# Three more key units and four more tiles as float16 pairs, and a running maximum read from PSUM

## The chip, the cores and the metric

The kernel runs on one core of one Trainium2 chip. The metric is the device time of one execution in microseconds; several executions are timed and their median is compared. One more execution is recorded with the hardware profiler, and the trace comes from that one.

## The reference

Agent attention over four batches of 11456 tokens with 128 features and 49 agents, and after it a mixture of eight experts, of which each token takes one. In short:

```python
scale = 1 / sqrt(128)
a2k = softmax(scale * agents @ k.T)          # 49 x 11456, per batch
agent_v = a2k @ v                            # 49 x 128
x = softmax(scale * q @ agents.T) @ agent_v  # 11456 x 128
e = argmax(normalized(x) @ normalized(expert_emb).T / tau)
g = softmax(...)[e]
out = g * (relu(x @ w1[e]) @ w2[e])          # w1: 128 x 1024, w2: 1024 x 128
```

All inputs and outputs are float32.

## The kernel before

**Units and tiles.** A batch is cut into 12 units: 11 of 128 partitions x 8 tokens and a rest of 96 x 2. A unit of keys, values or queries is loaded by one DMA of 512 KB on SP's queue. The second part of the kernel works in tiles of half a unit: 23 a batch, numbered t from 0, of 4 columns x 128 tokens each, the last one smaller. Batches are numbered b from 0, so the second batch is b = 1.

**Keys.** For each unit the scores of keys and agents are computed, kept in SBUF (tile s_u, filled by ACT), and a running maximum m_run over the units is kept by DVE. When all units of a batch are in, the maximum is made final (`k_max`), and then the value units use the kept scores (`k2_unit`). There are two ways for a unit. `k1_f32` transposes the keys on TensorE in float32 (line 436, 8 transposes into two PSUM banks), copies them to SBUF (lines 439 on DVE and 441 on ACT), multiplies with the agents in float32 (line 449; 16 matmuls a unit, of which the trace has two records each), copies the scores on ACT (473) and takes the maximum from PSUM on DVE (416). `k1_pairs` splits the keys into a float16 pair, value and residual, after a scaling by a power of two: ACT squares and sums them (490), DVE makes the scale (248, 250, 252), ACT writes the scaled value (494), DVE the residual (502). A DMA on SP's queue transposes both (507), and TensorE does three float16 matmuls for each of 8 columns (516 to 518). ACT copies the scores with the inverse scale (522), and the maximum is taken from that copy. Batches 0 and 1 use `k1_f32` alone. Of batches 2 and 3 `by_pairs` (line 1640) sends the even units through `k1_pairs`, the odd ones through `k1_f32`.

**Score banks.** Scores, routing sums and value sums go through a PSUM pool of two banks (tag s), and the transposes, the first layer and the proofs (vp) through one of four (tag h).

**Expert layers.** All tokens of a batch take, as far as can be proved, one expert, and what that expert does is folded beforehand (`pick_expert`) into small tables of that batch: gh and gl for the first layer, w2p for the second, lin for a linear part. Making them is a chain through ACT, DVE, TensorE and POOL, which runs beside the tiles of the batch before. For each tile and each of two blocks f, `ffn_mm1` does the first layer into an hp bank (1237, 1238) and the ReLU; `ffn_mm2` adds the second layer into yp. A tile is either a pair tile (ACT writes the float16 value, line 1246, DVE its residual, 1247; three float16 matmuls for each of 4 columns, 1273 to 1275) or a plain one (ACT writes float32, 1242; one float32 matmul for each column, 1270, two records each). `plain` (line 1223) makes tiles 16 and later plain, in all batches but the last.

**Order of the work.** The instructions are emitted by generators that a loop over ticks steps through, 4 ticks a tile, 92 a batch. `plan` gives due times to the key, value and query units: the keys of batch 2 begin at 0.30 of batch 0's ticks and those of batch 3 at 0.30 of batch 1's, spread evenly over 0.76 of a batch. From the emitted program a planner with estimated costs and priorities makes the order of each engine; SP's queue alone keeps the order of emission. Two buffers hold split keys (`h_slots`), three hold transposed ones (`x_slots`).

Of the kernel before, what the change touches and what calls it, by code (L numbers as in the profile page):

```python
# [14 lines left out]
ALU = mybir.AluOpType  # L15
# [14 lines left out]
def kernel(ctx: ExitStack, tc: tile.TileContext, q, k, v, agents, emb, tau, w1, w2, out):  # L30
    nc = tc.nc
    pe, dve, act, pool, sp = nc.tensor, nc.vector, nc.scalar, nc.gpsimd, nc.sync

    B, N, C = q.shape
    A = agents.shape[1]
    E, D, F = w1.shape
# [8 lines left out]
    BRISK = 4  # L45
    KEEP = 5
    LATE = 16

    REM_J, REM_P = 2, 96
    J = (N - REM_J * REM_P) // P  # L50
    TJ = 4
# [38 lines left out]
    def pss(name):  # L90
        return ps_s.tile([P, 512], F32, name=name, tag="s")
# [14 lines left out]
    def take(o, uses=1):  # L106
        at = o.asked
        o.asked += 1
        while len(o.left) < at or (at >= o.n and o.left[at - o.n]):
            yield 1  # L110
        o.left.append(uses)
        return at

    def give(o, i):
        o.left[i] -= 1
# [15 lines left out]
    def used(*unit):  # L131

        ring[slot[unit]][1] = now[0]
# [12 lines left out]
    def ushape(u):  # L146
        return (P, min(UJ, J - u * UJ)) if u < NU - 1 else (REM_P, REM_J)
# [94 lines left out]
    def half_scale(ssq, kexp, tag, bufs=2, bias=float(254 * ONE)):  # L242

        p = ssq.shape[0]
        sc = sm.tile([P, 1], F32, name="hsc", tag=tag + "c", bufs=bufs)[:p]
        iv = sm.tile([P, 1], F32, name="hiv", tag=tag + "i", bufs=bufs)[:p]
        si = sc.bitcast(I32)
        dve.tensor_scalar(si, ssq.bitcast(I32), -0.5, (190.5 + kexp) * ONE, ALU.mult, ALU.add)
        yield 1
        dve.tensor_scalar(si, si, EXPONENT, None, ALU.bitwise_and)  # L250
        yield 1
        dve.tensor_scalar(iv.bitcast(I32), si, -1.0, bias if isinstance(bias, float) else bias[:p], ALU.mult, ALU.add)
        return sc, iv
# [131 lines left out]
    def in_place(last):  # L385

        return tc.issue_after(last[-1].ins) if last else nullcontext()
# [20 lines left out]
    def blk_of(b, u):  # L408
        return [kb for kb in batches[b].blks if u in kb.us][0]

    def run_max(kb, spv, p, n):
        mr = kb.m_run[:p, :n, :]
        if kb.k1 + kb.us.start == 0:
            dve.tensor_copy(mr, spv)
        else:
            dve.tensor_tensor(out=mr, in0=spv, in1=mr, op=ALU.max)
# [61 lines left out]
    def k1_pairs(b, u):  # L478

        kb = blk_of(b, u)  # L480
        p, n = ushape(u)
        while ("k", b, u) not in units:
            yield 1
        src = units["k", b, u]
        kb.at[u] = yield from take(s_slots)
        j = yield from take(h_slots)
        sq = sm.tile([P, 1], F32, name="ksq", tag="ksq", bufs=3)[:p]
        xs = wk.tile([P, UJ, 2, D], F16, name="ks", tag="xs", bufs=XS)
        with in_place(h_last):
            act.activation(xs[:p, :n, 0], src[:p, :n], AF.Square, accum_out=sq)  # L490
        yield 1
        sc, iv = yield from half_scale(sq, 14, "ku", 4, kbias)
        with in_place(h_last):
            act.activation(xs[:p, :n, 0], src[:p, :n], AF.Copy, scale=sc)
        yield 1
        if u % 2:
            pool.tensor_tensor(out=src[:p, :n], in0=src[:p, :n], in1=sc.unsqueeze(2).broadcast_to([p, n, D]), op=ALU.mult)
            pool.tensor_tensor(out=xs[:p, :n, 1], in0=src[:p, :n], in1=xs[:p, :n, 0], op=ALU.subtract)
        else:
            for c in range(0, n, TJ):  # L500
                cs = slice(c, min(c + TJ, n))
                dve.scalar_tensor_tensor(out=xs[:p, cs, 1], in0=src[:p, cs], scalar=sc, in1=xs[:p, cs, 0], op0=ALU.mult, op1=ALU.subtract)
        used("k", b, u)
        yield 6
        i = yield from take(x_slots)
        kT = wk.tile([P, 2 * UJ, P], F16, name="kT", tag="xT", bufs=XB)
        sp.dma_start_transpose(out=kT[:, : 2 * n, :p], in_=xs[:p, :n].rearrange("p c h d -> p (c h d)"))
        yield 4
        give(h_slots, j)
        yield 1  # L510
        s = pss("sp")
        with in_place(y_last):
            for c in range(n):
                o = s[:p, c * A : (c + 1) * A]
                hi, lo = kT[:, 2 * c, :p], kT[:, 2 * c + 1, :p]
                pe.matmul(out=o, lhsT=hi, rhs=a16[:, b, :A], start=True, stop=False)
                pe.matmul(out=o, lhsT=hi, rhs=a16[:, b, A:], start=False, stop=False)
                pe.matmul(out=o, lhsT=lo, rhs=a16[:, b, :A], start=False, stop=True)
        give(x_slots, i)
        st = wk.tile([P, UJ, A], F32, name="s_u", tag="s_u", bufs=NU)[:p, :n]  # L520
        spv = s[:p, : n * A].rearrange("p (c a) -> p c a", a=A)
        act.activation(st, spv, AF.Copy, scale=iv)
        run_max(kb, st, p, n)
        kb.s[u] = st
        kb.k1 += 1

# [694 lines left out]
    live, yps = {}, {}  # L1221

    def plain(b, t):
        return b < B - 1 and t >= LATE

    def ffn_mm1(b, t, f):
        bt = batches[b]
        if plain(b, t) and not hasattr(bt, "w2f"):
            bt.w2f = sm.tile([P, 2, D], F32, name="w2f", tag="w2f", bufs=1)
            dve.tensor_tensor(out=bt.w2f, in0=bt.w2p[:, :, 0], in1=bt.w2p[:, :, 1], op=ALU.add)  # L1230
        u, w = unit_of(t)
        p, n = tshape(t)
        m = p * n
        tt = tts[b, u][:, w * TJ * P : w * TJ * P + m]
        hp = psh("hp")
        fs = slice(f * P, (f + 1) * P)
        pe.matmul(out=hp[:, :m], lhsT=bt.gh[:, fs], rhs=tt, start=True, stop=False)  # L1237
        pe.matmul(out=hp[:, :m], lhsT=bt.gl[:, fs], rhs=tt, start=False, stop=True)  # L1238
        h2 = wk.tile([P, 2, TJ * P], F16, name="hh", tag="hh", bufs=5)
        if plain(b, t):  # L1240
            hf = h2.rearrange("p h m -> p (h m)").bitcast(F32)
            h_last[:] = [act.activation(hf[:, :m], hp[:, :m], AF.Relu)]
            live[b, t, f] = (hf, None)
            return
        hh, hl = h2[:, 0], h2[:, 1]
        h_last[:] = [act.activation(hh[:, :m], hp[:, :m], AF.Relu)]  # L1246
        dve.scalar_tensor_tensor(out=hl[:, :m], in0=hp[:, :m], scalar=0.0, in1=hh[:, :m], op0=ALU.max, op1=ALU.subtract)  # L1247
        live[b, t, f] = (hh, hl)
# [389 lines left out]
        return sorted(kv), qs  # L1638

    def by_pairs(b, u):  # L1640
        return u % 2 == 0 and b > 1

    LEADS = {'k': 12, 'v': 9, 'q': 18}

# [13 lines left out]
    def keys():  # L1658

        start = now[0] // 2  # L1660
        for at, kind, b, u in plan()[0]:
            while now[0] // 2 < start + at:
                yield 1
            if kind == "k":
                if not hasattr(batches[b], "blks"):
                    k_start(b)
                spawn((k1_pairs if by_pairs(b, u) else k1_f32)(b, u))
            else:
                kb = batches[b].blks[0]
                if u == 0:  # L1670
                    while kb.k1 < NU:
                        yield 1
                    yield from k_max(b, pss, 1)
                    yield 1
                spawn(k2_unit(b, u, pool, (3, 4)))
                if u == NU - 1:
                    spawn(after_keys(b))
# [20 lines left out]
    with tc.manual_schedule(engines={mybir.EngineType.SP}):  # L1698
# [9 lines left out]
        for i in range(len(ticks) + LAG):  # L1708
            if i < len(ticks):
                b, t, r = ticks[i]  # L1710
# [12 lines left out]
            while due and due[0][0] <= i:  # L1723
                _, b, t, f = due.pop(0)
# [49 lines left out]
```

## Time and profile before

| what | value |
|---|---|
| median of 3 runs | 668.01 us (667.16 to 668.66) |
| profiled execution, its own time | 664.34 us |
| its span, first to last instruction | 662.6 us |
| TensorE (PE) busy | 631.3 us, 95% of the span |
| VectorE (DVE) busy | 513.8 us, 78% |
| ScalarE (ACT) busy | 458.7 us, 69% |
| GpSimd (POOL) busy | 345.7 us, 52% |
| mean granted TensorE clock | 0.996 |

The span is that of the instructions in the profiled execution; its own time has a little around it. The shares are averages over stages that differ. The end of a PE record is modelled and matmuls are pipelined, so the cost of a stream of matmuls is read from the starts of its records, not from their lengths.

### The profile page before, as it was taken

The numbers are of one execution on the slowest core, as the hardware profiler recorded it, in microseconds if no ns is written. First come the engines' busy times: TensorE is split into PE (matmuls) and PEld (weight loads), VectorE is DVE, ScalarE is ACT, GpSimd is POOL, SyncE is SP. The second block draws the span as 40 slices with busy tenths as digits, with TensorE's granted clock in tenths as the row PEclk, the third lists the DMA queues.
The fourth block names the chain that finished last, engine by engine and source line by source line (L and its number), as shares of the span: only waits on it lengthen the run. The fifth ranks groups of instructions, "written<-read, shape, count | busy, mean of one in ns | idle before, by whom it ended". The sixth has DMA issues, their size and how long they took to land. (4 is left out here: it accounts for less than half of the span.)

```text
span 662.6 us, 23329 instructions
## 1 busy us (share of the span) xinstructions
PE 631.3 (95%) x9299; PEld 540.1 (82%) x9299; DVE 513.8 (78%) x1487; ACT 458.7 (69%) x1147; POOL 345.7 (52%) x592
## 2 busy tenths in 40 slices
PE   8988999999999999999999889999999999999996
PEld 6887878888887877888888787888888897787886
DVE  5777798687776898876786889986576979896793
ACT  3537846877678956886777965876479855987642
POOL 6003284386135566783623684684655755877310
PEclk9989999999999999999999999999999999999999
DMA  8997397599686249999859455998568434314422
GB/s 341 286 348 212 57 342 194 125 226 286 180 265 188 64 118 217 285 295 230 216 182 245 120 114 147 264 282 217 130 196 216 102 65 138 62 34 137 142 101 76
DMA packets 157049, 123.33 MB, mean 186 GB/s; under 512 B 76753, under 2 KB 133155, under 8 KB 156939
## 3 DMA queue, kind: packets, MB, share of 16 engines
q1 hardware_dynamic: 143499, 97.97, 58.8%
q10 hardware_dynamic: 13120, 23.47, 10.2%
q8 instruction: 74, 1.21, 0.8%
q0 software_dynamic: 320, 0.38, 0.2%
q14 instruction: 36, 0.29, 0.1%
HBM read 80.26 MB, written 23.79 MB: 157 GB/s over the span
## 5 line engine op out<-in xcount | busy, mean ns | idle before, releaser
L1098 ACT ACTIVATE vp<-vp 128x512 f32<-128x512 f32 x180 | 106.4, 591 | 17.3 <-PE vp L1089 15.0
L1246 ACT ACTIVATE hh<-hp 128x512 f16<-128x512 f32 (+1 forms) x142 | 83.1, 592 | 47.9 <-PE hp L1238 32.6
L1247 DVE SCALAR_TENSOR_TENSOR hh<-hp,hh 128x512 f16<-128x512 f32 (+1 forms) x142 | 95.5, 676 | 26.3 <-ACT hh L1246 25.6
L1274 PE MATMUL yp<-w2p,hh 128*128 128x128 f16 x564 | 107.3, 219 | 0.0
L1273 PE MATMUL yp<-w2p,hh 128*128 128x128 f16 x564 | 107.0, 219 | 0.0
L1275 PE MATMUL yp<-w2p,hh 128*128 128x128 f16 x564 | 105.6, 219 | 0.3 <-DVE hh L1247 0.3
L449 PE MATMUL sp<-aT_all,fT 128*64 128x49 f32 x2496 | 95.9, 224 | 1.9 <-DVE vm L910 1.0
L449 PEld LDWEIGHTS sp<-aT_all,fT 128*64 128x64 f32 x2496 | 83.8, 137 | 15.9 <-issue 4.6
L441 ACT COPY fT<-fTp 128x512 f32<-128x512 f32 (+1 forms) x115 | 62.9, 572 | 31.1 <-PE fTp L436 20.7
L961 POOL TENSOR_TENSOR e<-qe,e 128x392 f16<-128x392 f32 (+1 forms) x48 | 43.0, 897 | 64.2 <-ACT e L958 53.0
L1237 PE MATMUL hp<-tt,gh 128*128 128x512 f16 (+1 forms) x184 | 68.7, 373 | 4.0 <-DVE hh L1247 1.8
L1089 PE MATMUL vp<-vm,tt 128*128 128x256 f16 x360 | 69.7, 273 | 0.7 <-DVE vmin L1095 0.6
L1036 POOL TENSOR_TENSOR nrm<-qq,half 128x16 f32<-128x16 f32 (+2 forms) x28 | 69.0, 2464 | 0.2
L1289 DVE TENSOR_TENSOR ot<-yp,gs 128x512 f32<-128x512 f32 (+1 forms) x92 | 61.5, 670 | 9.2 <-PE yp L1275 5.3
L1238 PE MATMUL hp<-tt,gl 128*128 128x512 f16 (+1 forms) x184 | 68.6, 373 | 0.0
L1261 PE MATMUL yp<-lin,tt 128*128 128x128 f16 x720 | 62.4, 219 | 2.2 <-DVE ot L1289 2.1
L1273 PEld LDWEIGHTS <-hh 128*128 128x128 f16 x564 | 55.4, 98 | 6.4 <-issue 0.7
L1275 PEld LDWEIGHTS <-hh 128*128 128x128 f16 x564 | 55.4, 98 | 6.1 <-DVE hh L1247 0.4
L1274 PEld LDWEIGHTS <-hh 128*128 128x128 f16 x564 | 55.5, 98 | 4.8 <-issue 0.5
L1261 PEld LDWEIGHTS <-tt 128*128 128x128 f16 x720 | 48.4, 99 | 9.9 <-issue 4.4
L997 POOL TENSOR_TENSOR rt<-rt 128x384 f32<-128x384 f32 (+1 forms) x48 | 40.7, 848 | 29.0 <-DVE rt L994 14.1
L436 PE MATMUL fTp<-ident,qt 128*128 128x128 f32 x360 | 54.2, 281 | 0.9 <-ACT vp L1098 0.4
(372 smaller groups left out, 1636.7 us busy)
## 6 DMA issues: line engine op xcount, KB each, us to landing
kt<-in_k_dram SPq DMA_DIRECT2D x44, 512.0 KB, 6.5
vt<-in_v_dram SPq DMA_DIRECT2D x44, 512.0 KB, 6.4
qt<-in_q_dram SPq DMA_DIRECT2D x44, 512.0 KB, 5.4
out_dram<-ot ACTq DMA_DIRECT2D x88, 256.0 KB, 3.5
w1s<-in_moe_w_dram SPq DMA_DIRECT2D x9, 512.0 KB, 4.2
w2s<-in_moe_w_dram SPq DMA_DIRECT2D x9, 512.0 KB, 5.3
tt<-e SPq DMA_TRANSPOSE x48, 4.6
kt<-in_k_dram SPq DMA_DIRECT2D x4, 96.0 KB, 8.5
```

The lines of the kernel that those rows point to most:

```text
L449: pe.matmul(out=s[h : h + w, c * A : (c + 1) * A], lhsT=xT[:, c * p + h : c * p + h + w], rhs=aT_all[:, b, :], start=True, stop=True, skip ...
L1036: pool.tensor_tensor(out=nrm, in0=quad, in1=half[:, :n], op=ALU.pow)
L1089: pe.matmul(out=z[:p, i * FP : (i + 1) * FP], lhsT=tt[:, c * p : (c + 1) * p], rhs=bt.vm[:, NEAR:], start=True, stop=True)
L1098: act.activation(z[:p], z[:p], AF.Relu, scale=-1.0, accum_out=bt.vsum[:p, at : at + 1])
L1237: pe.matmul(out=hp[:, :m], lhsT=bt.gh[:, fs], rhs=tt, start=True, stop=False)
L1238: pe.matmul(out=hp[:, :m], lhsT=bt.gl[:, fs], rhs=tt, start=False, stop=True)
L1246: h_last[:] = [act.activation(hh[:, :m], hp[:, :m], AF.Relu)]
L1247: dve.scalar_tensor_tensor(out=hl[:, :m], in0=hp[:, :m], scalar=0.0, in1=hh[:, :m], op0=ALU.max, op1=ALU.subtract)
L1261: pe.matmul(out=yp[:p, c, :], lhsT=tc_, rhs=bt.lin[:, h], start=(c == 0 and h == 0), stop=False, skip_group_check=True)
L1273: pe.matmul(out=y, lhsT=hh[:, cs], rhs=wh, start=False, stop=False, skip_group_check=True)
L1274: pe.matmul(out=y, lhsT=hh[:, cs], rhs=wl, start=False, stop=False, skip_group_check=True)
L1275: y_last[:] = [pe.matmul(out=y, lhsT=hl[:, cs], rhs=wh, start=False, stop=last, skip_group_check=True)]
```

## The change

Three edits. `MORE` names three odd units, unit 3 of batch 2 and units 3 and 7 of batch 3, which now go through `k1_pairs`; the branch of `k1_pairs` for odd units, which would have made the residual on POOL, goes, so all residuals are made on DVE. In `k1_pairs` the running maximum is taken from the scores in PSUM, scaled in the same instruction, and not from ACT's copy. And in batch 1 plain tiles begin at tile 20, so tiles 16 to 19 become pair tiles.

```diff
+    MORE = {2: (3,), 3: (3, 7)}
...
-        if u % 2:
-            pool.tensor_tensor(out=src[:p, :n], in0=src[:p, :n], in1=sc.unsqueeze(2).broadcast_to([p, n, D]), op=ALU.mult)
-            pool.tensor_tensor(out=xs[:p, :n, 1], in0=src[:p, :n], in1=xs[:p, :n, 0], op=ALU.subtract)
-        else:
-            for c in range(0, n, TJ):
-                cs = slice(c, min(c + TJ, n))
-                dve.scalar_tensor_tensor(out=xs[:p, cs, 1], in0=src[:p, cs], scalar=sc, in1=xs[:p, cs, 0], op0=ALU.mult, op1=ALU.subtract)
+        for c in range(0, n, TJ):
+            cs = slice(c, min(c + TJ, n))
+            dve.scalar_tensor_tensor(out=xs[:p, cs, 1], in0=src[:p, cs], scalar=sc, in1=xs[:p, cs, 0], op0=ALU.mult, op1=ALU.subtract)
...
         act.activation(st, spv, AF.Copy, scale=iv)
-        run_max(kb, st, p, n)
+        mr = kb.m_run[:p, :n, :]
+        if kb.k1 + kb.us.start == 0:
+            dve.tensor_scalar(mr, spv, iv, None, ALU.mult)
+        else:
+            dve.scalar_tensor_tensor(out=mr, in0=spv, scalar=iv, in1=mr, op0=ALU.mult, op1=ALU.max)
...
     def plain(b, t):
-        return b < B - 1 and t >= LATE
+        return b < B - 1 and t >= (LATE + 4 if b == 1 else LATE)
...
     def by_pairs(b, u):
-        return u % 2 == 0 and b > 1
+        return b > 1 and (u % 2 == 0 or u in MORE[b])
```

## Rows read from the trace of the kernel before

**Rows 1.** Busy us by stretch: PE, PEld, DVE, ACT, POOL; clock, DMA.
```profile
160.00:180.00 20.00, 20.00 (x318) 16.99 (x316) 15.09 (x36) 14.17 (x36) 6.37 (x12) 1.00 0.88 226
320.00:340.00 20.00, 20.00 (x338) 17.58 (x333) 16.70 (x38) 14.98 (x37) 8.94 (x11) 1.00 0.71 195
350.00:370.00 20.00, 19.01 (x245) 16.41 (x245) 12.15 (x43) 16.00 (x39) 9.68 (x13) 1.00 0.95 243
365.00:380.00 15.00, 12.96 (x155) 10.20 (x154) 12.58 (x29) 14.97 (x30) 10.36 (x11) 1.00 0.43 109
```

**Rows 2.** Timeline of ACT: start and length in us, then the instruction.
```profile
169.70 0.49 ACT L473 COPY s_u<-sp 128x392 f32<-128x392 f32 x1 [1.54 <-PE sp L449]
...
326.68 0.49 ACT L473 COPY s_u<-sp 128x392 f32<-128x392 f32 x1 [0.36 <-PE sp L449]
...
345.32 0.63 ACT L1242 ACTIVATE hh<-hp 128x512 f32<-128x512 f32 x1
...
363.57 0.61 ACT L1242 ACTIVATE hh<-hp 128x512 f32<-128x512 f32 x1
...
376.65 0.47 ACT L473 COPY s_u<-sp 128x392 f32<-128x392 f32 x1
```

**Rows 3.** Timeline of PE; 17 single rows stand between 360.24 and 360.71.
```profile
351.81 0.60 PE L436 MATMUL fTp<-ident,kt 128*128 128x128 f32 x4
352.25 0.55 PE L1261 MATMUL yp<-lin,tt 128*128 128x128 f16 x7
352.73 1.14 PE L449 MATMUL sp<-aT_all,fT 128*64 128x49 f32 x32
353.80 0.38 PE L258 MATMUL total<-wsq,ones 128*128 128x1 f32 x2
...
360.24 0.18 PE L516 MATMUL sp<-a,kT 128*128 128x49 f16 x1
...
360.71 0.38 PE L1237 MATMUL hp<-tt,gh 128*128 128x512 f16 x1
...
361.81 1.06 PE L1270 MATMUL yp<-w2f,hh 128*128 128x128 f32 x8
362.71 0.61 PE L1261 MATMUL yp<-lin,tt 128*128 128x128 f16 x8
363.15 0.38 PE L1237 MATMUL hp<-tt,gh 128*128 128x512 f16 x1
```

**Rows 4.** Busy us by stretch for tile ks (split keys) alone: DVE, ACT.
```profile
130.00:140.00 10.00, 1.42 (x2) 2.28 (x3) 1.00 0.75 207
...
370.00:380.00 10.00, 2.39 (x2) 0.68 (x1) 1.00 0.09 33
```

**Rows 5.** Groups by form: count, busy us, mean ns, idle before and its releaser.
```profile
L1247 DVE SCALAR_TENSOR_TENSOR hh<-hp,hh 128x512 f16<-128x512 f32 x140 | 94.8, 681 | 26.1 <-ACT hh L1246 25.6
...
L441 ACT COPY fT<-fTp 128x512 f32<-128x512 f32 x107 | 60.3, 591 | 30.5 <-PE fTp L436 20.7 <-PE hp L1238 3.0 <-DVE vmin L1171 1.8
...
L473 ACT COPY s_u<-sp 128x392 f32<-128x392 f32 x32 | 15.4, 485 | 16.0 <-PE sp L449 16.0
...
L522 ACT ACTIVATE s_u<-sp,hiv 128x392 f32<-128x392 f32 x12 | 7.1, 592 | 3.7 <-PE sp L518 3.7
```

**Rows 6.** The running maximum: its two groups by form; who waited for it.
```profile
L416 DVE TENSOR_TENSOR m_run<-sp,m_run 128x392 f32<-128x392 f32 x28 | 15.7, 562 | 12.3 <-ACT s_u L473 12.2
...
L416 DVE TENSOR_TENSOR m_run<-s_u,m_run 128x392 f32<-128x392 f32 x12 | 9.0, 746 | 1.1 <-ACT s_u L522 0.9
...
  PEld sp L449: 1.6, 3
```

**Rows 7.** What the first matmuls of pair units (L516) waited for.
```profile
  DMA kT<-ks: 3.1, 3
```

**Rows 8.** Waits of SP's queue: us in total, times, longest.
```profile
SPq L507 <- PE hp L1238: 17.5, 2, 11.5
```

**Rows 9.** Timeline of PE at the change to the third batch.
```profile
397.67 0.38 PE L1237 MATMUL hp<-tt,gh 128*128 128x512 f16 x1 [1.79 <-DVE hh L1247]
```

## The prediction

> **What bounds the kernel now.** I read the busy time by stretches first. TensorE (PE) is busy 20.00 of 20 us in 160 to 180 and in 320 to 340, while DVE and ACT have 3 to 6 us of rest [rows 1]: there the time is PE's instruction stream, and a microsecond of matmuls less is a microsecond less. It isn't so everywhere. In 365 to 380 ACT is busy 14.97 of 15 us and PE only 12.96 [rows 1]: this is the end of the second batch's second layer, where the third batch's expert is being picked. So each part of the change has to be placed before it is priced, and the second view is the ACT timeline, which dates the parts [rows 2]: the score copy (L473) of the third batch's unit 3 stands at 169.70, of the fourth batch's unit 3 at 326.68 and of its unit 7 at 376.65; the first ReLU of the second batch's tile 16 stands at 345.32, and of its tile 18 at 363.57. Then come the pitches of the PE instructions, by the starts of merged rows [rows 3], and the price of the same work on ACT and DVE [rows 4, 5].
>
> **The three units, on PE.** A float32 unit issues 8 transposes and 16 score matmuls (32 records). Four transposes take 352.25 - 351.81 = 0.44 us, so eight 0.88; the 32 score records take 353.80 - 352.73 = 1.07; together 1.95 us [rows 3]. A float16-pair unit issues 24 matmuls of 49 columns; 18 of them take 360.71 - 360.24 = 0.47 us, so 24 take 0.63 [rows 3]. Saved: 1.32 us of PE a unit, 3.96 us in all.
>
> **The three units, on the other engines.** ACT gives up one copy of 128x512 (0.59; the other half goes to DVE) and the score copy (0.49), and takes 2.28 for square, accumulator and scaled copy and 0.59 for the scaled score copy [rows 4, 5]: +1.79 us a unit. DVE gives up a copy of 128x512, which I price like L1247's pass over the same shape (0.68), and takes the two residuals: 1.42, or 2.39 where they collide with something [rows 4, 5]: +0.7 to +1.7 us, and three one-column instructions. In 160 to 180 and 320 to 340 both engines have room for that [rows 1]. Each unit also puts a transpose by DMA on SP's queue, and SP is in order: the twelve there now stood in it waiting for as much as 11.5 us at a time [rows 8], with the loads of later units behind them. PE pays where the transposed keys are late: 3.1 us over the twelve, weight loads and matmuls counted both, so about 1.5 us of PE time [rows 7]. At 0.13 us each three more cost +0.4; the bounds are 0 and the whole 1.5 again, and I take the mean, since most of the twelve weren't late at all (3 waits).
>
> **Where that lands.** The two units 3 lie where PE is full: -1.32 each. Unit 7 lies in the stretch that ACT fills: its PE saving counts nothing there. But its copies (0.59 + 0.49) leave that stretch, because a pair unit does its square and scaling some 20 us before its scores, in 350 to 360. I take half of these 1.08 us, -0.5; bounds 0 and -1.08 (all of it, if ACT alone sets the stretch).
>
> **The maximum from PSUM.** It reads the scores directly, but it doesn't get rid of the wait: the float32 units do it in this way already, and their maximum still stood 12.2 us behind ACT's copy of the same bank [rows 6]. What is left are two effects. The form with two SBUF operands lasts 746 ns on average, the PSUM form 562 [rows 6]: 12 x 0.184 = 2.2 us of DVE work less. The bounds on the path are 0 and -2.2; DVE isn't what most of the affected stretches wait for, and I take a quarter, -0.55. Against it, the score bank (one of two) is now free only after DVE. In the float32 units that held PE's weight loads for 1.6 us [rows 6], over the 36 float32 key units of the four batches; for 15 pair units at this rate +0.67 (bounds 0 and 1.6). [...] The rows of this kernel show the PSUM form no longer than the SBUF form, and the sum goes by them.
>
> **The four tiles.** A plain tile's second layer takes 2 x (362.71 - 361.81) = 1.80 us on PE; 24 float16 matmuls of 128 columns at (363.15 - 362.71) / 8 = 0.055 take 1.32 [rows 3]. Saved: 0.48 a tile, 1.92 in all. The ReLU on ACT has the same shape. DVE gets 8 residuals of 0.68, 5.4 us [rows 5], in a stretch of 28 us; in 350 to 370 it is idle for 7.85 of 20 us [rows 1], so they fit, but in order: each stands ahead of a link of the third batch's expert choice, which runs through DVE at the same time, and each holds an hp bank. Tiles 16 and 17 lie where PE is nearly full: -0.96. Tiles 18 and 19 lie with ACT: 0. The residuals cost between 0 and 5.4; the nearest row is a first-layer matmul that waited 1.79 us for one residual behind a full DVE queue [rows 9]. I take +0.7, some 0.1 us each, because DVE is idle for two fifths of the stretch where most of them fall.
>
> **The sum.** -1.32 - 1.32 - 0.5 - 0.55 - 0.96 + 0.4 + 0.67 + 0.7 = -2.9 us. The branch on POOL that goes away never ran (before, only even units were pairs). The profiled execution took 664.34 us (span 662.6 and 1.7 around it), so its like would take 661.4. It was faster than the three timed runs; against their median of 668.0 the change gives 665.1 us.
>
> **The rivals.**
> *PE's whole saving arrives.* All 3.96 + 1.92 = 5.9 us: 662.1. For it: PE is at or near its limit in four of the stretches. Against it: ACT is full in 365 to 380, where two fifths of the saving fall (unit 7, tiles 18 and 19: 2.28 of 5.9).
> *Nothing arrives*: 668.0. The shorter stream runs into what stood just behind it, ACT and the choice of the third batch's expert, and waits there for as long as it gained. For it: these lie right behind the tiles and unit 7. Against it: the saving at 169 lies 170 us ahead of that, and the choice itself starts earlier by it.
> *Slower, through DVE.* The eight residuals stand ahead of links of the third batch's expert choice, which PE awaits at the change of batches. All eight there are 5.4 us, against 2.64 us that the choice starts earlier: +2.8, 670.8. It decides from about four residuals (2.64 / 0.68) ahead of a link. For it: PE did wait for DVE at the change of batches [rows 9]. Against it: DVE has 7.85 us idle in 350 to 370 [rows 1].
> [...]
>
> **How the numbers follow.** The forecast has 0.47, the whole saving 0.15, nothing 0.20, the slower way through DVE 0.16, the weight loads 0.02. The order of the instructions comes from a planner, which may move much that isn't touched; I give the forecast 1.5 us either way for that, 663.6 to 666.6. Some 0.2%, 1.3 us, is what a measurement can tell from no change. Of the forecast 0.41 lies beyond that, and with the whole saving faster has 0.56; 0.06 of the forecast and 0.18 of nothing make same 0.24; 0.02 of nothing, 0.16 and 0.02 make slower 0.20. The range runs from 661.5, just past the whole saving, to 669.6, which takes in the weight loads and a part of the way through DVE.
>
> **What would show it.** Right: the float32 score records drop by 96, the records of the pair lines rise to 15 units, and the pitches stay; PE stays full in 160 to 180 and 320 to 340, and what follows comes earlier by 1.3 us after each; the maximum's wait for ACT's score copy now stands at the pair units; DVE's idle time around 350 to 370 shrinks by some 5 us. Wrong: the choice of the third batch's expert ends as late as now or later, PE waits longer at the change of batches, or new waits of PE for the transposed keys or for the score bank exceed 2 us.

## The result, and the profile after

The changed kernel takes 676.69 us (median of 4 runs, 675.6 to 677.55) against 668.34 for the kernel before on the same chip (4 runs): ratio 1.0119, 95% interval 1.0082 to 1.0157. It is slower by 8.4 us where 2.9 us faster was forecast, and lies outside the forecast range. Its profiled execution took 676.83 us, with a span of 675.1 and a mean granted clock of 0.985. The spans of the two profiled executions differ by 12.5 us, 4 more than the medians, since the profiled one of the kernel before took less than its median (664.34 us); so the traces are read for where time goes, and the medians for how much.

The work itself changed as forecast. Groups by form of the changed kernel (lines after `MORE` are one further down, those between the removed branch and the maximum three further up), which answer to [rows 5, 6]:

```profile
L1274 PE MATMUL yp<-w2p,hh 128*128 128x128 f16 x592 | 112.4, 220 | 2.5 <-ACT hh L1247 2.5
L450 PE MATMUL sp<-aT_all,fT 128*64 128x49 f32 x2368 | 91.2, 226 | 3.1 <-ACT sel L814 1.2 <-DVE vm L911 0.7 <-DVE m_run L417 0.7
L1271 PE MATMUL yp<-w2f,hh 128*128 128x128 f32 x224 | 30.7, 277 | 0.0
L491 ACT ACTIVATE ks<-kt 128x1024 f16<-128x1024 f32 x15 | 15.8, 1056 | 5.4 <-DMA kT<-ks 5.4
L417 DVE TENSOR_TENSOR m_run<-sp,m_run 128x392 f32<-128x392 f32 x25 | 14.1, 563 | 11.1 <-ACT s_u L474 11.0
L513 PE MATMUL sp<-a,kT 128*128 128x49 f16 x120 | 11.3, 185 | 0.2 <-DVE avx L557 0.2
L524 DVE SCALAR_TENSOR_TENSOR m_run<-sp,hiv,m_run 128x392 f32<-128x392 f32 x15 | 9.2, 616 | 1.0 <-ACT s_u L519 0.8
```

Float32 score records fell by 96 (2464 before), first matmuls of pair units rose from 96 to 120, records of plain tiles fell by 64 (288 before). The fourth row from the top has no like in the kernel before: the squares of the pair units (L491) waited 5.4 us for "DMA kT<-ks", the transposition of split keys.

Busy time by stretches, changed kernel (PE, PEld, DVE, ACT, POOL; clock; DMA), which answers to [rows 1]:

```profile
160.00:180.00 20.00, 20.00 (x326) 17.45 (x325) 17.61 (x42) 15.15 (x37) 7.28 (x11) 1.00 1.05 271
320.00:340.00 20.00, 19.78 (x333) 17.14 (x332) 16.73 (x38) 13.32 (x32) 11.05 (x19) 1.00 0.99 241
360.00:380.00 20.00, 16.16 (x190) 12.64 (x191) 14.49 (x43) 15.82 (x36) 9.24 (x12) 0.91 0.52 145
380.00:400.00 20.00, 14.32 (x175) 10.90 (x172) 16.33 (x45) 12.88 (x29) 10.86 (x21) 0.83 0.35 82
390.00:395.00 5.00, 3.83 (x22) 2.57 (x22) 3.15 (x15) 0.37 (x1) 2.73 (x2) 0.50 0.64 157
```

and the same two stretches of the kernel before:

```profile
360.00:380.00 20.00, 17.96 (x233) 14.59 (x229) 16.30 (x40) 19.97 (x42) 11.51 (x12) 1.00 0.50 135
380.00:400.00 20.00, 17.53 (x227) 15.52 (x225) 17.32 (x57) 13.54 (x35) 15.09 (x29) 1.00 0.55 122
```

PE is still full where it was full. Between 360 and 400 it has lost 35.49 - 30.48 = 5.0 us of busy time, and every other engine is less busy too: there all of them wait. The ACT timeline of the changed kernel says for what:

```profile
355.57 0.20 ACT L1099 ACTIVATION_READ_ACCUMULATOR vp<-vp 128x1 f32 x1
359.28 1.06 ACT L491 ACTIVATE ks<-kt 128x1024 f16<-128x1024 f32 x1 [3.52 <-DMA kT<-ks]
...
363.13 0.48 ACT L772 COPY sel<-gp 128x392 f32<-128x392 f32 x1
...
375.65 0.59 ACT L814 COPY sel<-row 128x512 f32<-128x512 f32 x1 [1.42 <-PE row L811]
378.08 1.06 ACT L491 ACTIVATE ks<-kt 128x1024 f16<-128x1024 f32 x1 [1.85 <-DMA kT<-ks]
...
379.14 0.56 ACT L814 COPY sel<-row 128x512 f32<-128x512 f32 x1
...
381.70 1.16 ACT L825 ACTIVATE sel<-sel,nkey 128x1024 f16<-128x1024 f32 x1
```

The same instructions of the third batch's expert choice in the kernel before:

```profile
358.48 0.47 ACT L771 COPY sel<-gp 128x392 f32<-128x392 f32 x1
...
370.56 0.60 ACT L813 COPY sel<-row 128x512 f32<-128x512 f32 x1
...
371.63 0.60 ACT L813 COPY sel<-row 128x512 f32<-128x512 f32 x1
...
372.58 1.19 ACT L824 ACTIVATE sel<-sel,nkey 128x1024 f16<-128x1024 f32 x1
```

There are two buffers for split keys. At 355.8 they held units 4 and 6 of the fourth batch; unit 4's transposition had been issued on SP at 350.18 and landed at 359.20, 9.0 us later (the 4.85 us of the row are the issue alone):

```profile
350.18 4.85 SPq L504 DMA_TRANSPOSE kT<-ks  x1
```

So the square of unit 7, a unit that used no such buffer before, stood at the head of ACT's queue for 3.52 us. ACT ran nothing else meanwhile: behind it stood the copy of gp, the start of the choice, whose matmuls were done at the same time in the changed kernel and in the one before (358.39 and 358.24):

```profile
356.51 1.88 PE L724 MATMUL gp<-avT,w1s 128*128 128x49 f32 x16
```

```profile
356.25 1.99 PE L723 MATMUL gp<-avT,w1s 128*128 128x49 f32 x16
```

The copy ran 4.65 us later than before. Only the last 0.9 us of the wait fell behind gp's matmuls; the other 3.8 us are ACT work that now stood ahead of the copy, unit 7's square and scaled copy among it. The square of unit 8 then waited 1.85 us between the two row copies, and the first ranking instruction on ACT ran 9.1 us late (381.70 against 372.58). What PE did meanwhile:

```profile
361.76 0.27 PE L1090 MATMUL vp<-vm,tt 128*128 128x256 f16 x1 [2.01 <-ACT vp L1099]
...
379.76 1.14 PE L450 MATMUL sp<-aT_all,fT 128*64 128x49 f32 x32 [1.17 <-ACT sel L814]
...
383.48 0.38 PE L1238 MATMUL hp<-tt,gh 128*128 128x512 f16 x1 [1.27 <-ACT hh L1243]
390.92 3.57 PE L839 MATMUL placed<-sel,gt 128*128 128x256 f16 x16 [3.38 <-DVE sel L831]
...
405.62 0.25 PE L1238 MATMUL hp<-tt,gh 128*128 128x192 f16 x1
```

PE ran nothing else either while it stood 3.38 us for the choice, and first layers of the second batch's last tiles came only behind that wait (the last one is at 405.62). The granted clock then was 0.50 in 390 to 395, where the 16 matmuls of `placed` took 3.57 us; with the clock at 1.00 the kernel before did 15 of them in 1.80:

```profile
383.36 1.80 PE L838 MATMUL placed<-sel,gt 128*128 128x256 f16 x15
```

ACT began to write the new table gh at 394.32 instead of 385.10.

### The profile page after: what moved, and what is told of

The parts are those of the page before. It is cut to its first block, busy times and chain, and to the rows that moved or that the text cites. A ratio compares the mean times of both kernels' runs of the same rounds, so it can differ in the third digit from the quotient of the medians.

```text
span 675.1 us, 23331 instructions
## 1 busy us (share of the span) xinstructions
PE 633.1 (94%) x9283; PEld 539.6 (80%) x9283; DVE 517.8 (77%) x1507; ACT 463.3 (69%) x1153; POOL 341.8 (51%) x592
## 5 line engine op out<-in xcount | busy, mean ns | idle before, releaser
L1248 DVE SCALAR_TENSOR_TENSOR hh<-hp,hh 128x512 f16<-128x512 f32 x150 | 101.1, 677 | 30.7 <-ACT hh L1247 29.9
L1247 ACT ACTIVATE hh<-hp 128x512 f16<-128x512 f32 x150 | 87.8, 590 | 43.4 <-PE hp L1239 22.8
L1274 PE MATMUL yp<-w2p,hh 128*128 128x128 f16 x596 | 113.1, 220 | 2.5 <-ACT hh L1247 2.5
L1275 PE MATMUL yp<-w2p,hh 128*128 128x128 f16 x596 | 113.2, 220 | 0.0
L1276 PE MATMUL yp<-w2p,hh 128*128 128x128 f16 x596 | 111.1, 220 | 0.7 <-DVE hh L1248 0.7
L450 PE MATMUL sp<-aT_all,fT 128*64 128x49 f32 (+1 forms) x2400 | 93.9, 226 | 3.1 <-ACT sel L814 1.2
L450 PEld LDWEIGHTS sp<-aT_all,fT 128*64 128x64 f32 (+1 forms) x2400 | 81.8, 139 | 16.4 <-issue 4.5
L442 ACT COPY fT<-fTp 128x512 f32<-128x512 f32 (+1 forms) x112 | 61.2, 571 | 25.9 <-PE fTp L437 17.5
L1274 PEld LDWEIGHTS <-hh 128*128 128x128 f16 x596 | 59.1, 99 | 9.1 <-ACT hh L1247 3.0
L1276 PEld LDWEIGHTS <-hh 128*128 128x128 f16 x596 | 58.7, 99 | 6.3 <-DVE hh L1248 0.9
L1275 PEld LDWEIGHTS <-hh 128*128 128x128 f16 x596 | 58.7, 99 | 2.9 <-issue 0.3
```

Of the source, the lines that this page charges most:

```text
L450: pe.matmul(out=s[h : h + w, c * A : (c + 1) * A], lhsT=xT[:, c * p + h : c * p + h + w], rhs=aT_all[:, b, :], start=True, stop=True, skip ...
L1274: pe.matmul(out=y, lhsT=hh[:, cs], rhs=wh, start=False, stop=False, skip_group_check=True)
L1275: pe.matmul(out=y, lhsT=hh[:, cs], rhs=wl, start=False, stop=False, skip_group_check=True)
L1276: y_last[:] = [pe.matmul(out=y, lhsT=hl[:, cs], rhs=wh, start=False, stop=last, skip_group_check=True)]
```

## The experiments

Theory A: the waits for a split-key buffer, at the head of ACT's queue, carry the loss. B: the tiles' residuals on DVE do. C: the planner's order alone, with no one wait. D: the maximum from PSUM carries it by itself. E: a coupling of the three edits at the end of the second batch. F: a DVE instruction of the choice is held by POOL's instructions. Medians are set against the kernel before on the same chip (668.8 to 670.1 in the first twelve, 666.93 in the last three).

**One edit at a time.** Three units only (`plain` and the maximum as before), the maximum only (`MORE` empty, `plain` as before), the tiles only:

```diff
-    MORE = {2: (3,), 3: (3, 7)}
+    MORE = {2: (), 3: ()}
```

Units: 

> The kernel before with the three more pair units alone (maximum from the copy, tiles 16 to 19 of the second batch plain). Theory A, split-key buffers: with units 3 and 4, 7 and 8 in a row the square of a later pair unit (fourth batch's unit 7) waits on ACT for one of the two split-key buffers, ACT's queue stands still for some 3.5 us there, and the third batch's expert choice behind it comes 4 to 6 us late: this kernel is slower than before by 4 to 9 us, and its trace shows the wait of ks for the DMA kT<-ks. Theory B, residuals: the eight DVE residuals of the four tiles delay the choice: this kernel is 1 to 4 us faster than before, as the units save PE time. Theory C, the planner's new order alone: anything within 4 us either way, without a wait for the buffers in 355 to 380.

Maximum: 

> The kernel before with the maximum from PSUM alone. Theories A and B: within 1.5 us of before (a little less DVE work, banks held longer). Theory C: up to 4 us either way, as any edit that changes the planner's order.

Tiles: 

> The kernel before with the second batch's tiles 16 to 19 as pairs alone. Theory A: within 2 us of before (1 us of PE saved, up to 2 us lost to residuals). Theory B: slower by 4 to 9 us, the choice of the third batch's expert late by as much. Theory C: up to 4 us either way.

Measured: units 0.996 (0.9922 to 0.9999), maximum 1.005 (1.0014 to 1.0086), tiles 0.9975 (0.9942 to 1.0008). Together they would give 0.9985; the change is at 1.0119. B falls with the tiles, and D can explain some 0.5% (0.9% by its interval). A's forecast for the units, 4 to 9 us slower, missed, though they have the same two waits of ACT (3.54 us before the square at 361.17, 1.39 before the one at 385.90). But there gp's own matmuls ended only at 361.9, so the first wait held up nothing that was ready, and the second stands behind the first ranking instruction (375.82).

**Two edits at a time, and the change without unit 7.**

```diff
-    MORE = {2: (3,), 3: (3, 7)}
+    MORE = {2: (3,), 3: (3,)}
```

Without unit 7: 

> The changed kernel without the fourth batch's unit 7 among the pairs (its unit 3 and the third batch's unit 3 stay). Theory A: the wait of about 3.5 us for the buffer at 355 to 360 goes, the choice of the third batch's expert comes 4 to 6 us earlier, and the time falls by 4 to 8 us against the changed kernel, to within 3 us of before. Theory B: no faster than the changed kernel by more than 1.5 us. Theory C: anything, and the choice's lateness not tied to the wait.

Units and tiles: 

> The change without the maximum from PSUM: three more units and the four tiles. Theory D, the maximum: it alone carries the loss (as a sole edit it was 0.5% slower), so this kernel is 3 to 6 us faster than before, as the sum of the units alone and the tiles alone. Theory E, coupling at the end of the second batch: units and tiles together put too much ahead of the third batch's expert choice, PE's idle time there grows by 5 us or more over before, and the kernel is 2 to 7 us slower than before.

Units and maximum: 

> The change without the tiles. Theory D: the sum of the parts alone, about -3 + 3 = 0 us, within 2 us of before. Theory E: the same or a little better, since the residuals are gone; the choice of the third batch's expert no later than 4 us against before.

Maximum and tiles: 

> The change without the units. Theory D: the sum of the parts alone, about +3 - 1 = +2 us (0 to +4). Theory E: at least 5 us slower, if it is the maximum's and the residuals' DVE work that meet there; no more than 2 slower if the units are needed for it.

Measured: without unit 7 1.0091 (1.0049 to 1.0133), units and tiles 1.0074 (1.004 to 1.0108), units and maximum 1.0199 (1.0144 to 1.0255, 4 runs), maximum and tiles 1.005 (1.0021 to 1.0079). Two edits that are each below 1 cost 0.7% together, as E forecast, and units and maximum read worse than all three, which neither D nor E did. A's forecast for the kernel without unit 7, 4 to 8 us faster than the changed one, missed too: its squares wait for no buffer, and it is still 0.9% slower than before. That looked like C or E; the traces show a second mechanism. In the kernel with units and maximum, DVE, POOL and PE:

```profile
370.60 0.34 POOL L994 TENSOR_TENSOR rt<-qe 96x98 f32<-96x98 f32 x1
370.69 8.27 DVE L762 TENSOR_SCALAR nkey<-key 128x8 f32<-128x8 f32 x1
370.91 2.03 POOL L799 TENSOR_TENSOR sel<-ident,key 128x512 f32<-128x512 f32 x2
372.90 1.82 POOL L819 TENSOR_TENSOR gt<-gts,gt 128x392 f16<-128x392 f32 x2
374.69 2.03 POOL L751 TENSOR_TENSOR w2s<-w2s,hsc 128x512 f32<-128x512 f32 x2
376.68 2.25 POOL L752 TENSOR_TENSOR w1s<-w2s,w1s 128x512 f16<-128x512 f32 x2
379.61 1.01 PE L1262 MATMUL yp<-lin,tt 128*128 128x128 f16 x8 [9.25 <-DVE ot L1290]
```

An instruction over 8 elements a partition lasts 8.27 us: it ends at 378.96, when POOL's four steps, one right behind the other, have ended (378.93). DVE stands still so long, and PE has a hole of 9.25 us. Without unit 7 it lasts 9.20. The kernel before:

```profile
366.97 0.34 POOL L993 TENSOR_TENSOR rt<-qe 96x98 f32<-96x98 f32 x1 [0.99 <-DVE hsc L250]
367.19 0.16 DVE L761 TENSOR_SCALAR nkey<-key 128x8 f32<-128x8 f32 x1
367.27 2.03 POOL L798 TENSOR_TENSOR sel<-ident,key 128x512 f32<-128x512 f32 x2
```

starts it 80 ns ahead of the four steps and takes 0.16 us; the changed kernel starts it 50 ns ahead of them (at 373.28) and takes 0.17 us. What decides isn't shown, since in the kernel before, too, POOL had a short instruction under way (0.34 us, begun 220 ns earlier). In units and maximum the hold lasted over four pairs of POOL instructions.

**A control for moves of the order.** The kernel before with one DVE memset of one column, in the third batch's unit 0:

```diff
-        sc, iv = yield from half_scale(sq, 14, "ku", 4, kbias)
+        sc, iv = yield from half_scale(sq, 14, "ku", 4, kbias); b == 2 and u == 0 and dve.memset(sm.tile([P, 1], F32, name="nop", tag="nop", bufs=1), 0.0)
```

> The kernel before with one added DVE memset of one column at the third batch's first pair unit: no work to speak of (under 0.1 us), but the planner's order changes in places behind it. If the planner's order alone can move the time (theory C), this kernel differs from before by 1 us or more either way; if not, by less than 0.7 us.

Measured: 1.0003 (0.9963 to 1.0043). This move of the order changed nothing that can be measured; the interval, 2.7 us either way, doesn't exclude the 1 us that C asked for.

**The hold taken away.** nkey by the form that also sums:

```diff
-            dve.tensor_scalar(nkey, key, -1.0, None, ALU.mult)
+            dve.tensor_scalar(nkey, key, -1.0, 0.0, ALU.mult, ALU.add, accum_out=sm.tile([P, 1], F32, name="nks", tag="nks"))
```

Units and maximum: 

> Units and maximum (1.020 of before) with nkey's instruction in another form: it also sums its output, which is a form that in these traces was never held (L822 ran 1.27 us each time, beside POOL too). Theory F, DVE held by POOL: in the kernel of units and maximum the 128x8 nkey took 8.27 us, from 370.69 to just behind POOL's row of eight products without a pause, and PE stood 9.25 us. With the other form nkey takes some 0.2 us, that hole of PE closes, and the kernel is 6 to 10 us faster than units and maximum, 0.995 to 1.010 of before. Theory A, buffers, alone: no change, within 2 us. Theory C: anything.

Without unit 7: 

> The changed kernel without the fourth batch's unit 7 (1.009 of before; its nkey took 9.20 us), with nkey in the form that sums. Theory F: nkey takes 0.2 us and the kernel is 6 to 10 us faster than that one, 0.993 to 1.000 of before. Theory A alone: no change, as no wait for buffers was left in it.

The kernel before: 

> The kernel before with the negated key alone made by the summing form: the control. Theory F: in the kernel before the instruction starts 80 ns ahead of POOL's run and isn't held in the third batch's choice, so 0.997 to 1.003. If it comes out at 0.995 or less, the gains seen with this form belong to the form in any kernel, and not to a hold that the change brought.

Measured: units and maximum 1.0081 (1.0043 to 1.012), 1.2% below the same kernel with the old form; without unit 7 1.0055 (1.0021 to 1.0088), 0.4% below, with intervals that overlap; the kernel before 1.0023 (0.9998 to 1.0049), so the form is no gain of itself. In the first of them

```profile
371.25 0.16 DVE L762 TENSOR_SCALAR_CACHE_REDUCE nkey<-key 128x8 f32<-128x8 f32 x1
```

lasts 0.16 us instead of 8.27, and F is shown for this pair. Without unit 7, where it lasts 0.16 us too and starts 30 ns after POOL's line 994, F's forecast of 6 to 10 us missed. The hole of 7.67 us that PE had for DVE is gone there, but a later DVE entry beside POOL's run (367.61 to 376.53), a pair of residuals, is long instead.

```profile
372.05 5.69 DVE L499 SCALAR_TENSOR_TENSOR ks<-kt,hsc,ks 128x512 f16<-128x512 f32 x2
```

```profile
379.53 1.95 PE L450 MATMUL sp<-aT_all,fT 128*64 128x49 f32 x32 [3.77 <-DVE m_run L524]
```

Such a pair takes 1.40 to 2.06 us in the changed kernel. PE's hole of 3.77 us behind it can explain why little came back there; no run took this second delay away. F isn't the cause in the changed kernel, where nkey isn't held in the third batch's choice and no DVE instruction of the whole trace lasts longer than 1.40 us.

**The buffer wait taken away.** The whole change, but unit 7 of the fourth batch splits its keys in a buffer of the load ring:

```diff
-        j = yield from take(h_slots)
+        own = (b, u) == (3, 7)
+        if not own:
+            j = yield from take(h_slots)
+        while own and not room():
+            yield 1
...
+        if own:
+            xs = big("ks").bitcast(F16).rearrange("p c (h d) -> p c h d", h=2)
+            j = len(ring) - 1
...
+        if own:
+            ring[j][1] = now[0]
...
```

The whole change: 

> The changed kernel in which the fourth batch's unit 7 has its split keys in a buffer of the load ring, and not in one of the two split-key buffers. Theory A, split-key buffers: ACT's waits for kT<-ks of 3.5 us before unit 7's square and 1.8 us before unit 8's go, the third batch's expert choice has its gh 4 to 8 us earlier by the tiles before it, and the kernel is 4 to 8 us faster than the changed one. If nkey then falls behind the start of POOL's row, theory F takes it back: nkey of 8 to 9 us in the trace, and no gain. Theory C: no tie to the waits.

With the summing form as well: 

> Both: unit 7's split keys in the load ring, and nkey in the form that sums. Theories A and F together: neither the waits for buffers nor a held nkey, the end of the second batch costs what it does in the kernel before, and PE's saving is left: 1 to 5 us faster than before (0.993 to 0.999). Theory C: between before and the changed kernel.

Without the maximum: 

> The three units and the four tiles without the maximum from PSUM (that form: 1.0074), with the fourth batch's unit 7 splitting its keys in a buffer of its own. Theory A (the square of unit 7 and of unit 8 waiting for a split-key buffer at the head of ACT's queue): 5 to 8 us come back, ratio 0.990 to 0.997, and no wait of ACT for the keys' transposition over 0.5 us between 355 and 385. Theory D (the maximum costs by itself what the buffers don't): this kernel is faster than the one with the maximum and the own buffer (0.9994) by 0.3% or more. Theory C (the planner's order alone): still 1.004 or more.

Without the maximum, with the summing form: 

> The same with the negated key of the expert choice made by the summing form, which POOL doesn't hold. Theory F (a DVE instruction of the choice held by POOL's run) expects this to be the fastest of all, 0.985 to 0.995, if the hold occurs in the kernel without it, and no change to that kernel if it doesn't. Theory C: 1.00 or more.

Measured: 0.9994 (0.9956 to 1.0032); 0.9982 (0.994 to 1.0023); 0.9994 (0.9957 to 1.0031); 0.9998 (0.9971 to 1.0025). From the changed kernel that is 1.2% or 8 us back, as A forecast, and from units and tiles (1.0074) 0.8% or 5 us. None of the four is shown to be faster than the kernel before, which A and F had forecast for the second (0.993 to 0.999) and A for the third (0.990 to 0.997). ACT in the first of these kernels, which does the same instructions:

```profile
357.49 1.05 ACT L499 ACTIVATE ks<-kt 128x1024 f16<-128x1024 f32 x1
...
361.32 0.49 ACT L783 COPY sel<-gp 128x392 f32<-128x392 f32 x1
...
365.28 1.07 ACT L499 ACTIVATE ks<-kt 128x1024 f16<-128x1024 f32 x1
...
374.41 0.58 ACT L825 COPY sel<-row 128x512 f32<-128x512 f32 x1 [0.82 <-PE row L822]
375.77 0.58 ACT L825 COPY sel<-row 128x512 f32<-128x512 f32 x1 [0.78 <-PE row L822]
376.43 1.15 ACT L836 ACTIVATE sel<-sel,nkey 128x1024 f16<-128x1024 f32 x1
```

Neither square waits, and unit 8's runs 12.8 us earlier; the ranking starts 5.3 us earlier, though this run was 2.6 us behind the kernel before already at the ranking of the first choice (67.8, against 65.2). No instruction that the change touches runs up to there; the mean granted clock of the whole run was 0.987, against 0.996. Its stretches 360 to 380 and 380 to 400, in the columns of the windows above, and its `placed`:

```profile
360.00:380.00 20.00, 16.73 (x257) 13.56 (x256) 18.19 (x46) 18.29 (x36) 10.98 (x13) 1.00 0.64 169
380.00:400.00 20.00, 17.65 (x195) 15.47 (x195) 17.48 (x53) 14.30 (x36) 14.77 (x27) 0.91 0.35 75
```

```profile
387.22 1.91 PE L850 MATMUL placed<-sel,gt 128*128 128x256 f16 x16
```

In the two stretches PE is busy 34.38 us with 452 matmuls; the kernel before has 35.49 and 460, the changed one 30.48 and 365.

The time from the end of gp's last matmul to the first ranking instruction on ACT tells the kernels apart:

| kernel | us | ratio |
|---|---|---|
| before | 14.3 | 1 |
| units; maximum; tiles, each alone | 13.9; 14.4; 15.2 | 0.996; 1.005; 0.9975 |
| own buffer, with and without the maximum | 16.2; 16.9 | 0.9994; 0.9994 |
| changed; units and tiles; units and maximum with the summing form | 23.3; 23.1; 23.1 | 1.0119; 1.0074; 1.0081 |
| units and maximum | 32.0 | 1.0199 |

In the three of the fourth row ACT waits for the buffers on this stretch of the chain; in the last one the hold comes on top.

So A is shown, with and without the maximum. The two waits aren't priced one by one, and the order of ACT's work moved with them (unit 8's square is now ahead of the ranking). D falls as the cause of the whole loss: with the own buffer the kernels with and without the maximum are both at 0.9994. E holds in so far as the wait costs only with other edits beside it. C isn't excluded for what is left. No kernel beats the one before by more than can be measured, except perhaps the three units alone (0.996, whose interval ends just below 1).

## Why the prediction was wrong

**Units on PE: right.** In 160 to 162 of the changed kernel 24 pair matmuls run in 161.30 - 160.68 = 0.62 us, 0.63 was forecast, and the records fell as above. Alone, the units measured 2.7 us faster (5.2 to 0.1), and their terms -1.32 - 1.32 - 0.5 + 0.4 make 2.7; with an interval so wide, and the two buffer waits in that kernel, the agreement may be luck.

**Tiles on PE: right.** A pitch of 0.055 again (eight matmuls from 161.52 to 161.96). By counts and pitches PE's stream is shorter by the 5.9 us that were forecast in all (an estimate). The span grows by 12.5 all the same: PE stands outside its busy time for 662.6 - 631.3 = 31.3 us before and for 675.1 - 633.1 = 42.0 after, and where the clock was 0.50 its records last longer (the 16 of `placed`, 3.57 us). Nor did the third batch's choice start earlier by the 2.64 us that I counted on: gp's matmuls end at 358.39, against 358.24.

**Unit 7 (-0.5) and the late transposed keys (+0.4): this is the step that failed.** I placed unit 7's square and scaling "in 350 to 360" (they ran at 359.28 and 362.09) and priced only what leaves the later stretch. I priced the late keys as a wait of PE, by [rows 7]. PE didn't wait for them at all (no such entry at L513). They were late for the next user of the buffer: a unit's buffer is held from the square until its transposition has read it out (unit 4: from 329.98, when its square starts, to 359.20, which is 29 us, 20 of them until the transposition is issued), and with two buffers a third pair unit must wait for the first. The two waits came to 5.4 us (3.52 and 1.85), on ACT, ahead of links of the chain that PE awaits; with their knock-on (the work that piled up on ACT, the row copies, in this trace the clock of 0.50 in 390 to 395) they are worth the 8 us that the own buffer gives back. The rest of the miss, some 2.5 us from 0.9994 to the forecast, is the saving that doesn't arrive even then (below). The number of these buffers stood in the description of the kernel, and I didn't ask who would wait for one. I named what was queued behind the transposition on SP, not what was queued behind the square on ACT.

**Residuals of the tiles (+0.7): not the loss.** The tiles alone are at 0.9975 (0.9942 to 1.0008), where -0.96 + 0.7 would be 0.9996.

**Maximum (-0.55 and +0.67): right in kind, open in size.** It lasts 0.616 us instead of 0.746, and 0.562 was assumed; it still waits for ACT's copy, as forecast (0.8 us); PE's weight loads waited 1.2 us for it and the float32 form together, no more than the 1.6 of [rows 6]. These durations give a small gain, and only against a mean: of the twelve in the kernel before, seven took 0.548 to 0.568 us and five 0.657 to 1.260, and the new form takes 0.562 to 0.625, so it gains on the five and loses a little on the seven. Alone the maximum measured 0.5% or 3.4 us slower, with the own buffer nothing. Where the 0.5% comes from stays open.

**The rivals.** "Slower, through DVE" named the right place, the third batch's choice, and the wrong engine and cause. The sign given that the choice ends later, and PE waits longer, came true. "Nothing arrives" describes the kernel with the own buffer by its number; that the gain is lost in the way it tells isn't shown. The 0.02 on weight loads, and their part in the range: no run shows that they set PE's pitch, and the pitches stayed (24 pair matmuls in 0.62 us, 0.055 for 128 columns).

**What stays open** is why PE's 5.9 us don't show even then. One part is seen: at the second batch's choice ACT waits for that batch's weights at the head of its queue, in the kernel before and in the one with the own buffer:

```profile
188.27 1.06 ACT L731 ACTIVATE sel<-w1s 128x1024 f16<-128x1024 f32 x1 [1.49 <-DMA w1s<-in_moe_w_dram]
```

```profile
192.76 1.06 ACT L743 ACTIVATE sel<-w1s 128x1024 f16<-128x1024 f32 x1 [3.42 <-DMA w1s<-in_moe_w_dram]
```

That is 1.9 us more. But the kernel without the maximum hasn't this wait, and its median is the same. In the kernel without the maximum and with the summing form the first output tile of the fourth batch is computed 4.3 us earlier than in the kernel before, and the last one 0.7: the gain is given back in the fourth batch, in waits of a microsecond and less and in work that was put off, of which none stands out. And runs of one kernel spread: the kernel without the maximum, with the own buffer, took 664.0 to 673.9 us at mean granted clocks of 0.994 down to 0.980. The intervals here reach 0.25 to 0.56% either way, and not the 0.2% that I assumed, so that a gain of 2 us would hardly be told.

## What to carry to other kernels

Whoever sends more work through a ring of buffers should price the ring before the work: how long one buffer is held (here 29 us from the square to the landing of the transposition), how many users come within that time, and which engine's queue the first writer stands in, with everything behind it. Three edits that alone measured between 0.4% faster and 0.5% slower cost 1.2% together: the wait for the buffer cost nothing that could be seen where nothing ready stood behind it, and 8 us where the choice did; so test the sum, and look in the trace for engines that are all less busy at once. And a profile in which a short instruction takes microseconds is to be read with the neighbour engine's rows beside it.

## What the runs showed of the hardware

A DVE TENSOR_SCALAR over 128x8 took 0.16 us when it started 80 ns ahead of a POOL run, and 8.27 and 9.20 us in two kernels in which POOL had begun a short instruction (0.34 us, line 994) 90 and 30 ns before it and went on to its run. Both ended within 0.03 us of the end of POOL's last step. In the kernel before the like of that instruction had begun 220 ns before it (366.97) and held nothing, so the exact condition stays open. The summing form took 0.16 us, also where it started 30 ns behind that short instruction (without unit 7, 367.33 and 367.30).

And in the changed kernel a hole of PE came with a lower clock behind it: PE stood for 3.38 us up to 390.92, the granted clock was 1.00 in 384 to 389 and 0.50 in 390 to 395, and 16 matmuls took 3.57 us there that took 1.91 in the kernel with the own buffer, and 15 of them 1.80 at 1.00 in the kernel before. Not every hole does: before the matmul at 192.19 PE stood for 1.90 us in the same kernel, and the granted clock was 1.00 in 192.2 to 205.
